# A recurrent attention block and a gated feed-forward on one core: a new list schedule, merged gram products, and y turned by transposes

## The chip, the core and the metric

The kernel runs on one core of a Trainium2 chip. Its five engines work side by side: PE (TensorE, matrix products), DVE (VectorE), ACT (ScalarE), POOL (GpSimd) and SP (SyncE, which here issues nearly all the transfers). Each engine takes its instructions in a fixed order and waits on semaphores for what others make. The metric is the time of one execution on the device in microseconds, as a median of the runs shown; lower is better.

## The reference

For 32 independent sequences (4 batches of 8 heads), with 768 tokens and a head size of 40, a 40 x 40 state is updated token by token. The output of all heads then goes through a normalised gated feed-forward.

```python
for t in range(S):
    y[:, :, t] = einsum('bhd,bhde->bhe', rt, state)
    Sa = einsum('bhde,bhe->bhd', state, at)
    state = state * wt[..., None, :] - einsum('bhd,bhe->bhde', Sa, bt) + einsum('bhd,bhe->bhde', vt, kt)
x = y as (B*S, H*D)                       # 3072 x 320
xn = x / sqrt(mean(x*x) + 1e-6) * rms_g
out = (silu(xn @ w_gate) * (xn @ w_val)) @ w_out     # 320 -> 1536 -> 320
```

r, k, v, w, a, b and the results are float32. The feed-forward's weights arrive as float64 and are narrowed in the kernel.

## The kernel before

The tokens are cut into 24 chunks of 32 (`C = 32`). Each chunk passes through three stages, and each pair of chunks (`CG = 2`) through a fourth.

- `front(c)` loads the chunk, turns it by transposes (`turned`, line 371), and climbs a ladder of five levels, `LEVELS = (1, 2, 4, 8, 16)`. A level makes one gram product of K with A (32 small products on PE, lines 546 to 550, recorded at line 368), copies part of it into the triangular matrix LT under a mask (`where`, a predicated copy on DVE), and makes K and A of the next level by scaling one half of each block (DVE, line 324) and copying the other half (ACT, line 348). At levels 1 and 2 the product takes 16 columns (`ps<-A,K`), at the other three 56 (`ps<-Ab,K`). Then LT goes through DRAM (sB) into another layout (M).
- `inverse(c)` inverts the triangle in 31 steps of two DVE instructions each (`tmp`, `Yi`), and sends it through DRAM (sY) back into LT.
- `main(c)` carries the state: X from the old state (`ST,aP`) and the values (`VU,LT`), then U (`Xs,LT`), then the update of ST (`VU,KN`). It also forms the scores (`rE,vut`), scales them into As, adds up five levels of products (`As,KN`, `As,kbn`) and the old state's part (`rE,Sd`, `r,Sd`) in y, turns y by 16 small products with the identity (`ps<-ident,y`, 32 records), normalises it to x, and turns that into xg.
- `feed(g)` runs the feed-forward of two chunks over 12 tiles of 128 hidden columns: the hidden products (`ps<-xg,wf`), Silu on ACT (sg), their product on DVE (hT), and the output products (`po<-wf,hT`). The narrowed weights (sW, in DRAM, made by `narrow` at the start) are loaded again for each pair into five buffers wf.

A product of float32 operands has two records of MATMUL and two of LDWEIGHTS in the trace; a transpose has one of each.

None of this is issued as it is written. Each step becomes a `Piece` with an engine, an estimated time and a due time, and `Plan.issue` (line 124) simulates the engines and writes the instructions out in the order in which it started them. The order is then fixed. Due times are written as offsets from the start of a chunk, which come every `T = 46.0`:

```python
due = d + 5 + 7.5 * j
pe(due - 14.5, 0.95, [mm(gr[half(i), o, n, 0:wide], K[...], side(A, l, 1)[...] if l <= 2 else A[..., 16:]) ...
```

On PE the planner also counts columns against a clock that it takes to be halved when there are too few, and puts in warming products (`plan.warm`, line 812, `po<-ident`) at the start. It counts transfers as one lane of 220 GB/s with fixed times around it. PSUM results are placed in three pairs of banks (`plan.room`).

Of the kernel before, what the change touches and what calls it, by code (L numbers as in the profile page):

```python
# [16 lines left out]
P = 128  # L17
C = 32
# [3 lines left out]
T = 46.0  # L22
N0, NF = -10.0, 6.0
S0, S1 = 15.0, 5.0
LAG = 10.0
M40 = 0.75
EARLY = 3
EPS = 1e-6


class Piece:


    def __init__(self, engine, due, time, issue, lane=0.0, columns=0, paced=False, room=None, since=0.0, tiled=None, many=0):
        self.engine, self.due, self.time, self.issue = engine, due, time, issue
        self.lane, self.columns, self.paced, self.room = lane, columns, paced, room
        self.many = many
        self.tiled = not columns if tiled is None else tiled
        self.ready, self.missing, self.users = since, 0, []


class Plan:
# [3 lines left out]

    LATENCY, SELF, MARGIN = 0.18, 0.115, 1.0
    SWITCH, STICK = 0.1, 3.0  # L50
    WINDOW, ENOUGH, KEEP = 3.41, 1600, 1300

    LINE, FETCH, STALL = 256, 3.6, 5.0
    LOOK, LOW = 1.0, 1300
    AHEAD, FAR = 2.0, 30.0
    WARM, FILL = 230.0, 1300

    def __init__(self, pairs, stand_ins):
        self.pieces = []
        self.seen = {}  # L60
        self.pairs, self.stand_ins = pairs, {t.tensor.name: t for t in stand_ins}
        self.now = {n: None for n in self.stand_ins}
        self.rooms = []

# [7 lines left out]
    def box(self, ap):  # L72
        dims = list(ap.ap)
        if ap.tensor.space == DRAM and ap.tensor.name not in self.now:

            g = all(s == 1 or s % 128 == 0 for s, n in dims) and [n for s, n in dims if s == 1] or [128]
            p = ap.offset % 128
            p, g = (p, g[0]) if p + g[0] < 128 else (0, 128)
            return p, p + g, ap.offset, ap.offset + sum(s * (n - 1) for s, n in dims) + 1
        row = dims[0][0]  # L80
        p, f = divmod(ap.offset, row)
        return p, p + dims[0][1], f, f + sum(s * (n - 1) for s, n in dims[1:]) + 1

    def add(self, engine, due, time, issue, outs, ins, **kw):
        me = len(self.pieces)
        piece = Piece(engine, due, time, issue, **kw)
        needs = set()
        mine = {}
        for aps, write in ((ins, False), (outs, True)):
            for ap in aps:  # L90
                name = ap.tensor.name
                a = self.box(ap)
                if name in self.now:
                    piece.room = self.now[name]
                    name = piece.room
                    a = 0, 128, *a[2:]
                if (name, write) in mine:
                    b = mine[name, write]
                    a = min(a[0], b[0]), max(a[1], b[1]), min(a[2], b[2]), max(a[3], b[3])
                mine[name, write] = a  # L100
        for (name, write), a in mine.items():
            left = []
            for b, i, w in self.seen.get(name, ()):
                if i != me and (write or w) and a[0] < b[1] and b[0] < a[1] and a[2] < b[3] and b[2] < a[3]:
                    needs.add(i)
                if not (write and a[0] <= b[0] and b[1] <= a[1] and a[2] <= b[2] and b[3] <= a[3]):
                    left.append((b, i, w))
            left.append((a, me, write))
            self.seen[name] = left
        piece.missing = len(needs)  # L110
# [3 lines left out]

# [9 lines left out]
    def issue(self):  # L124
        P_ = self.pieces
        waiting = {p.engine: [] for p in P_}
        free = {e: 0.0 for e in waiting}
        pairs = [0.0] * len(self.pairs)
        held, pace, left = [], 0.0, sum(p.paced is None for p in P_)
        clock, columns, recent, lane, order, full, line = [0.5], {}, [], 0.0, [], False, (0, -9.0)  # L130

        def put(i):
            p = P_[i]
            (held if p.paced and p.due > pace + self.FAR else waiting[p.engine]).append(i)

        def clock_at(t):
            while len(clock) <= int(t / self.WINDOW):
                c = columns.get(len(clock) - 1, 0)
                clock.append(1.0 if c >= (self.ENOUGH if clock[-1] < 1 else self.KEEP) else 0.5)
            return clock[int(t / self.WINDOW)]  # L140

        def fill(t):
            nonlocal line
            line = (line[0] + 4) % self.LINE, (t if line[0] + 4 >= self.LINE else line[1])
            order.append((t, None))
            end = t + 0.214 / clock_at(t)
            w = int(t / self.WINDOW)
            columns[w] = columns.get(w, 0) + 256
            recent.append((t, end, 256))
            return end  # L150

        def at_least(i):
            p = P_[i]
            return max(p.ready, min(pairs)) if p.room is not None and self.rooms[p.room][1] is None else p.ready

        for i, p in enumerate(P_):
            if not p.missing:
                put(i)
        for _ in P_:
            t, e = min((max(free[e], min(at_least(i) for i in w)), e) for e, w in waiting.items() if w)  # L160
            can = [i for i in waiting[e] if at_least(i) <= t]
            if e == "PE":
                since = max(free[e], 3.0)
                while t < self.WARM and since + 0.3 < t:
                    since = fill(since)
                t = max(t, since)
                since = t + self.LOOK - self.WINDOW
                recent = [r for r in recent if r[1] > since]
                had = sum(r[2] * (r[1] - max(r[0], since)) / (r[1] - r[0]) for r in recent)
                many = [i for i in can if not P_[i].tiled or P_[i].columns >= 1000]  # L170
                if many and (clock_at(t) < 1 or had < self.LOW):
                    can = many
                else:
                    can = [i for i in can if not P_[i].paced or P_[i].due <= pace + self.AHEAD] or can
                    while clock_at(t) == 1 and had < self.FILL:
                        t = fill(t)
                        had += 256
                at = int(t / self.WINDOW)
                clock_at(t)
            if e == "PE":  # L180
                def run(p):

                    time = (p.time + (self.SWITCH if p.tiled == full else 0)) / clock[at]
                    end, left, done, begun, lost = t, p.many, line[0], line[1], 0.0
                    while done + left >= self.LINE:
                        n = self.LINE - done
                        end += time * n / p.many
                        lost += max(0.0, begun + self.FETCH - end)
                        end = begun = max(end, begun + self.FETCH)
                        left, done = left - n, 0  # L190
                    return end + time * left / p.many, (done + left, begun), lost
                runs = {i: run(P_[i]) for i in can}
                i = min(can, key=lambda i: (P_[i].due + (self.STICK if P_[i].tiled == full else 0) + self.STALL * runs[i][2], i))
            else:
                i = min(can, key=lambda i: (P_[i].due, i))
            waiting[e].remove(i)
            p = P_[i]
            end = t + p.time
            if e == "PE":
                end, line, _ = runs[i]  # L200
                full = not p.tiled
                over = min(1.0, max(0.0, (end - (at + 1) * self.WINDOW) / (end - t)))
                columns[at] = columns.get(at, 0) + p.columns * (1 - over)
                columns[at + 1] = columns.get(at + 1, 0) + p.columns * over
                recent.append((t, end, p.columns))
            free[e] = end
            if p.lane:
                lane = max(lane, end + 1.2) + p.lane
                end = lane + 1.0
            if p.room is not None:  # L210
                room = self.rooms[p.room]
                if room[1] is None:
                    room[1] = min(range(len(pairs)), key=lambda q: pairs[q])
                    pairs[room[1]] = float("inf")
                room[0] -= 1
                if not room[0]:
                    pairs[room[1]] = end + self.LATENCY
            order.append((t, i))
# [626 lines left out]
```

## Time and profile before

| what | value |
|---|---|
| median of 3 runs | 1265.81 us (1259.08 to 1271.15) |
| profiled execution: span on the core | 1281.1 us |
| PE busy | 1152.5 us, 90% |
| DVE busy | 887.6 us, 69% |
| ACT busy | 467.3 us, 36% |
| mean granted clock of PE | 0.938 |
| `ps<-A,K`, 16 columns | 3072 records, 59.7 us busy |
| `ps<-Ab,K`, 56 columns | 4608 records, 90.5 us busy |
| `ps<-ident,y` | 768 records, 16.3 us busy |
| warming products `po<-ident` | 698 records, 93.7 us busy |

The profile was taken from one execution with the hardware profiler. Only its span is given; no separate time of the same execution is. Busy times of PE are modelled at their ends and records of neighbours overlap, so the sum of groups is larger than the time that they occupy. A granted clock of 0.5 means that PE runs at half its speed in that stretch. "DVE hT L324: 21.9, 23, 2.4" in a list of waits is the total in us, the count and the longest.

### The profile page before, as it was taken

To read this page: it belongs to the slowest core of one execution; us is meant where nothing else is said; L and a number is where in the kernel's file an instruction comes from. 1 tells how busy PE (TensorE), PEld (TensorE's weight loads), DVE (VectorE), ACT (ScalarE), POOL (GpSimd) and SP (SyncE) were. 2 spreads that over 40 slices of the span, in tenths; PEclk is the share of its full clock that TensorE was granted. 3 is DMA by queue.
4 is the path that set the end of the run, shared out by engine and by line. 5 is a ranking of instruction groups with operands and counts; after the bars stand their busy time and mean duration, and the time that the engine had idled before them with its cause. 6 is when DMAs were issued, how large, how long until landed. Compare 5 with 4: busy or idle time off the path is not lost.

```text
span 1281.1 us, 58318 instructions
## 1 busy us (share of the span) xinstructions
PE 1152.5 (90%) x25626; PEld 937.6 (73%) x25626; DVE 887.6 (69%) x3012; ACT 467.3 (36%) x1060; POOL 47.3 (4%) x118
## 2 busy tenths in 40 slices
PE   7998769998998999988998998988999998999997
PEld 7898667777776777776777676777777776777775
DVE  5778986868768578677678677667677677577311
ACT  3734554334233334333333333334333333331111
POOL 5000000000000000000000000000000000000000
PEclk9999668999898899999999997989999998999999
DMA  7656664535535435535535535435436545333342
GB/s 105 138 151 161 155 178 80 132 84 120 118 80 133 102 98 133 105 99 131 116 80 136 117 85 129 108 85 140 100 92 141 115 99 121 101 91 92 95 143 61
DMA packets 307902, 145.77 MB, mean 114 GB/s; under 512 B 270784, under 2 KB 284608, under 8 KB 307648
## 3 DMA queue, kind: packets, MB, share of 16 engines
q1 hardware_dynamic: 297856, 140.57, 46.2%
q8 instruction: 201, 3.29, 1.1%
q10 hardware_dynamic: 9792, 1.48, 0.8%
q14 instruction: 53, 0.43, 0.1%
HBM read 125.83 MB, written 16.12 MB: 111 GB/s over the span
## 4 chain that ended last, share of the span: by engine, by line
PE 44%; DVE 26%; SPq 12%; DMA 9%; issue 5%; ACT 3%; POOL 0%; DVEq 0%; POOLq 0%; ACTq 0%
PE ps L368 29%; SPq L365 12%; PE po L368 8%; DVE tmp L324 5%; DVE Yi L324 5%; PE ps L371 4%; PE po L812 4%; DMA M<-sB 3%; DVE As L324 3%; DVE hT L324 2%; DVE K L324 2%; DVE LT L324 2%; DVE y L324 2%; DMA sW<-hT 1%; DMA kbn<-in_k_dram 1%
## 5 line engine op out<-in xcount | busy, mean ns | idle before, releaser
L368 PE MATMUL ps<-xg,wf 128*128 128x256 f32 (+1 forms) x1728 | 382.0, 410 | 12.7 <-DMA wf<-sW 5.3
L368 PEld LDWEIGHTS ps<-xg,wf 128*128 128x128 f32 (+1 forms) x1728 | 274.2, 198 | 69.1 <-issue 11.0
L368 PE MATMUL po<-wf,hT 128*128 128x320 f32 x576 | 199.0, 470 | 23.0 <-DVE hT L324 21.9
L324 DVE TENSOR_TENSOR tmp<-Yi,M 128x60 f32<-128x60 f32 (+24 forms) x744 | 156.5, 210 | 40.5 <-DMA M<-sB 23.0
L324 DVE TENSOR_TENSOR Yi<-Yi,tmp 128x60 f32<-128x60 f32 (+24 forms) x744 | 156.0, 210 | 18.2
L344 ACT ACTIVATE sg<-ps 128x256 f32<-128x256 f32 x144 | 55.2, 384 | 270.5 <-PE ps L368 268.9
L368 PEld LDWEIGHTS po<-wf,hT 128*128 128x128 f32 x576 | 102.1, 196 | 70.2 <-DVE hT L324 30.8
L348 ACT COPY KN<-ps 128x640 f32<-128x640 f32 x96 | 66.4, 692 | 169.8 <-DVE LT L324 68.1
L324 DVE TENSOR_TENSOR hT<-ps,sg 128x256 f32<-128x256 f32 x144 | 60.6, 421 | 97.4 <-ACT sg L344 97.1
L368 PEld LDWEIGHTS ps<-Ab,K 40*64 40x64 f32 x4608 | 80.2, 143 | 36.1 <-issue 19.3
L348 ACT COPY K<-K 128x256 f32<-128x256 f32 x240 | 91.1, 415 | 31.8 <-PE ps L368 26.1
L368 PE MATMUL ps<-Ab,K 40*64 40x56 f32 x4608 | 90.5, 229 | 13.1 <-ACT K L348 6.2
L324 DVE TENSOR_TENSOR K<-K,T 128x512 f32<-128x512 f32 (+1 forms) x192 | 93.3, 490 | 9.6 <-ACT K L348 9.4
L812 PE MATMUL po<-ident 128*128 128x128 f32 x698 | 93.7, 293 | 6.6 <-POOL eye L421 5.2
L812 PEld LDWEIGHTS po<-ident 128*128 128x128 f32 x698 | 88.1, 206 | 7.9 <-POOL eye L421 5.2
L324 DVE COPY_PREDICATED LT<-msk,ps 128x256 f32<-128x256 uint32 x120 | 66.1, 551 | 32.3 <-PE ps L368 21.2
L324 DVE TENSOR_TENSOR As<-ps,msi 128x512 f32<-128x512 f32 (+1 forms) x192 | 80.1, 484 | 7.3 <-PE ps L368 7.3
L368 PEld LDWEIGHTS ps<-As,KN 128*40 128x40 f32 x3072 | 67.5, 128 | 22.8 <-issue 7.1
L368 PE MATMUL ps<-As,KN 128*40 128x32 f32 x3072 | 73.8, 208 | 6.7 <-DVE hT L324 5.8
L368 PEld LDWEIGHTS ps<-A,K 40*64 40x64 f32 x3072 | 54.5, 145 | 26.1 <-issue 15.8
L368 PE MATMUL ps<-A,K 40*64 40x16 f32 x3072 | 59.7, 214 | 7.1 <-issue 3.1
L324 DVE TENSOR_TENSOR y<-y,ps 128x256 f32<-128x256 f32 x120 | 50.6, 421 | 19.8 <-PE ps L368 17.4
(106 smaller groups left out, 1321.0 us busy)
## 6 DMA issues: line engine op xcount, KB each, us to landing
wf<-sW SPq DMA_DIRECT2D x144, 480.0 KB, 4.5
M<-sB SPq DMA_DIRECT2D x96, 128.0 KB, 2.8
sW<-hT SPq DMA_DIRECT2D x24, 240.0 KB, 3.4
wan<-in_w_dram SPq DMA_DIRECT2D x48, 80.0 KB, 3.1
wan<-in_a_dram SPq DMA_DIRECT2D x48, 80.0 KB, 3.5
wn<-in_w_dram SPq DMA_DIRECT2D x96, 40.0 KB, 2.7
rn<-in_r_dram SPq DMA_DIRECT2D x24, 160.0 KB, 5.3
wf<-in_moe_w_out_dram SPq DMA_DIRECT2D x12, 320.0 KB, 3.4
```

Of the source, the lines that this page charges most:

```text
L324: plan.add("DVE", due, time + 0.00104 * size(o), lambda at: fn(at(o), *m(at)), [o], aps(*args))
L344: plan.add("ACT", due, 0.08 + 0.00083 * size(o), lambda at: nc.scalar.activation(at(o), at(a), f, **kw), [o] + aps(acc), [a])
L348: plan.add("ACT", due, 0.08 + 0.00083 * size(o), lambda at: nc.scalar.copy(at(o), at(a)), [o], [a])
L365: plan.add(by, due, 0.45, lambda at: queue.dma_start(out=o, in_=i), [o], [i], lane=max(0.4, n * 4 / 220e3), since=since)
L368: return o, lhsT, rhs, lambda at: nc.tensor.matmul(at(o), lhsT, rhs, start=start, stop=stop, skip_group_check=True), 4
L371: return o, i, ident, lambda at: nc.tensor.transpose(at(o), i, ident), 2
L812: plan.warm = lambda: nc.tensor.matmul(po_[:, 0, DM:DM + P], ident, ident, start=False, stop=False, skip_group_check=True)
```

## The change

It has three parts.

1. **The planner is rewritten.** A product's time, its drain when the kind of tiling changes, and the delay until others see it now come from a table by kind (`PRODUCTS`), and every transfer's time to landing from another (`LOADS`). The planner models blocks of 256 instructions on PE, up to 8 transfers in flight, and dependencies by exact elements instead of boxes. Due times come from a long table (`DUE`), one number for each piece of each stage, with separate rows for the first and last chunks; the choice among ready pieces weighs due time against start time (`KEEN`), a change of tiling (`STICK`) and an instruction-block stall (`LOSS`). `T` is 43.36 and warming products may come until 199 on the planner's time instead of 230.
2. **The ladder's levels 1 and 2 share one gram product.** A holds seven columns for each block of four tokens, in a tile of 16 x 8 x 7: the last three as they are, two and one times the decay. One product of 56 columns then gives the entries at distances 1, 2 and 3 inside a block of four, and three predicated copies with new masks (`near`) take them into LT. Level 2's factor is applied to K in place, and A for level 4 is made directly.
3. **The sequences' slots are reordered** (`slot(n) = n % 4 * 2 + n // 4`) in LT, K, A, ST and KN, and **y is turned by four full transposes** instead of 16 small products with the identity.

In the instructions: of each of 24 chunks' products, 32 of 16 columns go, 32 others of 16 become 56 wide, and 16 products for y become 4 transposes. PE has 397 warming products instead of 349. DVE has 57 instructions more in the whole program, ACT 120 fewer, POOL three Memsets more (A, and two of y). SP issues 1410 transfers as before, in another order.

```diff
-T = 46.0
+T = 43.364560000000004
+WARM = 199.0
+PRODUCTS = {
+    "out": (0.915, 0.359, 0.434, 0, 2560), "h": (1.618, 0.306, 0.381, 0, 4096), ...
+LOADS = {
+    "sB": (1.5, 0.1), "LT": (1.65, 0.15), "M": (2.6, 0.65), "sY": (2.3, 0.47), "wf": (3.85, 2.05), ...
+DUE = {
+    ("", 0): """-596 -468 -407 -645 -502 -1178 -655 -103 -167 -101 -269 -259 -795 ...
...
+                    p, t = P_[i], max(at, free[e])
+                    score = p.due + keen[e] * (t - free[e])
+                    if e == "PE":
+                        if p.mode != mode:
+                            score += stick
+                        if best is None or score < best[0]:
+                            score += stall * lost(p, at)
...
+            if p.load:
+                at = max(free[e], at)
+                free[e] = at + self.ISSUE
+                server = max(server, at + self.BEGIN) + p.load[1]
+                end = behind[e] = max(server, at + p.load[0], behind[e] + self.BEHIND)
+                landed.append(end)
...
-        copy(d, by_i(Tl[1]), ps[:, :, :, 0])
-        A = A_.next()
-        copy(d, by_i(A), ps[:, :, :, 1])
+        copy(by_i(Tl[1]), ps[:, :, :, 0])
+        A, Ab = A_.next(), Ab_.next()
+        copy(A[:, :, :, 0:3], a4.rearrange("p n (g j) -> p n g j", j=4)[:, :, :, 1:4])
+        copy(Ab[:, :, 0:C]...[:, :, :, :, 0], a4...[:, :, :, :, 0])
...
+        tt(A[:, :, :, 3:5], A[:, :, :, 1:3], w4[:, :, :, 1:3], MUL)
+        tt(A[:, :, :, 6], A[:, :, :, 4], w4[:, :, :, 1], MUL)
+        gr = plan.room().rearrange("p o (n t) -> p o n t", n=N)
+        pe("gramk", [mm(gr[half(i), o, n, 0:56], K[part(o), 2 * n + i].rearrange("p x s -> p (x s)"),
+                        A[part(o), 2 * n + i].rearrange("p g j -> p (g j)")) for n, i, o in each])
+        for dist, at in ((1, 0), (2, 3), (3, 6)):
+            m = 4 - dist
+            where(LT...[:, :, :, dist:], near[:, dist - 1:dist]...[:, :, :, dist:]..., g4[:, :, :, at:at + m])
...
-        for j, l in enumerate(LEVELS):
+        for j, l in list(enumerate(LEVELS))[2:]:
...
-                dma(due, sB[seq(i, q, o)]..., LT[rows(i, 1 - q), o * N + 4 * q:o * N + 4 * q + 4])
+                dma(sB[seq(i, q, o)]..., LT[rows(i, 1 - q), o * N + q:(o + 1) * N:2], "sB")
...
-        xn = plan.room()
-        pe(d + 42.7, 0.6, [mm(xn[half(q), o, m * D:(m + 1) * D],
-                            y[part(o), 2 * (q * 4 + m):2 * (q * 4 + m) + 2].rearrange("p i t -> p (i t)"),
-                            ident[part(o), part(o)]) for m in range(4) for q in range(2) for o in range(2)])
-        xv = xn[:, :, 0:4 * D]
+        xn = plan.room()[:, 0].rearrange("p (m c) -> p m c", m=4)
+        pe("turn4", [flip(xn[:, m], y.rearrange("p (m c) t -> p m (c t)", m=4)[:, m], ident) for m in range(4)])
+        xv = xn.rearrange("p m (o e) -> p o m e", o=2)[:, :, :, 0:D]
```

## The prediction

> **What bounds the kernel now.** I read the page first: the busy shares, the clock row and the chain that ended last.
>
> ```profile
> span 1281.1 us, 58318 instructions
> PE 1152.5 (90%) x25626; PEld 937.6 (73%) x25626; DVE 887.6 (69%) x3012; ACT 467.3 (36%) x1060; POOL 47.3 (4%) x118
> PEclk9999668999898899999999997989999998999999
> PE 44%; DVE 26%; SPq 12%; DMA 9%; issue 5%; ACT 3%; POOL 0%; DVEq 0%; POOLq 0%; ACTq 0%
> q8 instruction: 201, 3.29, 1.1%
> ```
>
> PE is busy 90% and idle 128.6 us. The chain is PE for 44% of the span and changes hands often: PE is nearly full, with many short waits. The dip in the clock row lies at 120 to 210 us. So next I cut the span at 213.54 us, where the first output product of feed(0) begins.
>
> ```profile
> 0.00:213.54 213.54, 177.03 (x3624) 165.00 (x3624) 165.17 (x509) 107.35 (x220) 20.35 (x55) 0.85 0.62 142
> 213.54:1281.15 1067.61, 975.47 (x22008) 772.63 (x22002) 722.39 (x2503) 359.90 (x840) 26.96 (x63) 0.96 0.45 108
> 150.00:200.00 50.00, 36.02 (x903) 32.86 (x905) 45.79 (x139) 29.61 (x64) 2.03 (x4) 0.70 0.70 172
> 622.00:668.00 46.00, 42.69 (x1041) 34.03 (x1040) 34.17 (x121) 16.73 (x41) 0.70 (x2) 1.00 0.47 111
> ```
>
> After the length, the columns are busy PE, weight loads, DVE, ACT, POOL, the clock, the DMA share and GB/s. In the first stretch PE's 177 us contain the warming products (row po<-ident, 93.7 us in the whole run); DVE is the full engine, 45.8 of 50 us. In the second, 1067.6 us, PE is idle 92.1. A mean clock of 0.96 with states of 1.0 and 0.5 means some 85 us at half speed, of which about 43 us are lost. So 92 + 43 = 135 us of the second stretch are not work at full speed. I look at who causes them, and at one case.
>
> ```profile
> PE po L368 <- DVE hT L324: 21.9, 23, 2.4
> PE ps L368 <- issue: 21.6, 24, 3.7
> PE ps L368 <- DVE y L324: 13.0, 19, 3.2
> PE ps L368 <- DVE hT L324: 9.3, 12, 1.9
> ...
> 1070.30 0.69 PE L368 MATMUL ps<-Xs,LT 32*32 32x40 f32 x53
> 1074.72 0.47 PE L368 MATMUL ps<-Xs,LT 32*32 32x40 f32 x11 [3.73 <-issue]
> 1075.12 3.78 PE L368 MATMUL ps<-xg,wf 128*128 128x256 f32 x8
> ```
>
> No wait is long; they come from products that stand too close behind what they need. The last three rows show a stall's second price: after 3.73 us without work, eight products take 3.78 us. The same eight take 1.89 at full clock (timeline at 621.45), so the stall cost 1.9 us more.
>
> **The sum, part by part.** For PE I use the time from one group's start to the next group's start, since records of neighbours overlap.
>
> ```profile
> 619.91 0.68 PE L368 MATMUL ps<-ident,y 40*64 40x40 f32 x32
> 620.52 1.09 PE L371 MATMUL ps<-ident,wan 128*128 128x128 f32 x8
> 621.45 1.89 PE L368 MATMUL ps<-xg,wf 128*128 128x256 f32 x8
> ...
> 630.53 1.12 PE L368 MATMUL ps<-A,K 40*64 40x16 f32 x64
> 631.59 0.26 PE L368 MATMUL ps<-Xs,LT 32*32 32x40 f32 x4
> ```
>
> *Grams.* Per chunk the build has 32 fewer gram instructions: two products A,K with 16 columns become one with 56. A,K takes 631.59 - 630.53 = 1.06 us for 64 records. The merged form stands in the trace as Ab,K, 56 columns, also x64: 607.29 to 608.44 with a start-to-start near 1.0 to 1.1. Width costs nothing here, count does. Saved: 24 x 1.06 = 25 us, on the bounding engine.
>
> *y.* 32 records in 0.61 us become four transposes. Eight transposes take 621.45 - 620.52 = 0.93, so four take 0.47. Saved: 24 x 0.14 = 3 us. Here a rule speaks against the change: the Trainium skill, "TensorE: Matmul & The Clock Gate", Part 4 (PE-mode transpose), says that transposes do not count as busy for the clock gate as other products do. By it, every chunk could lose one more window: a clock dip in this trace lasts at least 3.4 us and loses 1.7, so 24 x 1.7 = 41 us. The row against it is 622 to 668: it holds several groups of eight transposes (two in a row at 644.28 to 646.2) and has clock 1.00. I take 0 and keep the 41 us for the range.
>
> *Instruction blocks.* The q8 row is 201 blocks of 16.4 KB; with 2 x 25626 records that is 255 instructions a block. The Trainium skill, "Runtime: NRT & Kernel Launch" (Instruction fetch mechanics), says blocks of 256 instructions are fetched ahead and crossing one is mostly hidden. By the rule the 21.6 us of "issue" waits are something else and fewer instructions win nothing; by the trace each long one ends just before the next block's fetch, and no two fetches start within 3.3 us, while 128 gram instructions run in 1.06 us. I follow the trace. The build has 8.2% fewer PE records (23514), so 184 blocks: -2 us by count alone; the rest depends on how wide products are mixed in.
>
> *DVE and ACT.* Per chunk DVE loses two predicated copies (551 ns each), A<-A (420) and two Ab<-A (291 each). It gains three predicated copies of 128, 256 and 384 elements (on average the same 551, so 1653), two products on A (291 and 420) and two on Ab of 192 elements (about 356 between the rows of 128 and 256). Net +0.97 us, 23 us in all. Hidden: DVE is busy 722 of 1068 us; it would be 745 of about 960, 78%. Uncovered it costs the 23 us. ACT loses A<-ps 585, A<-A 429, two Ab<-A at 312, four K<-K at 415 and gains about 1.37 us (three wider copies): -1.9 us per chunk, off PE's path but one link of two in the gram ladder goes. POOL gains three Memsets (896 and twice 512 elements, by the rows of 1024 and 512 about 1.9 us) behind the others at 18 us, ahead of the first gram: at most 2 us once. Slot order and strided LT pieces keep the same 128-byte rows and the same 1410 SP issues: 0.
>
> *New order.* No view shows it, so I count in the build: PE work, at this trace's start-to-start times, between a product and the one that needs it. Medians before to after: X to U 2.8 to 11.4 us; scores to first level 2.7 to 4.3; last level to y 2.2 to 4.7; y to x 2.5 to 4.1; hidden products to the output product 2.7 to 3.4, with 56 of 144 closer than 2 us before and 33 after. Changes between full and tiled products fall from 471 to 441. At one end, nothing is won (a fixed order misses real landings); at the other all 135 us but the final 8 us go, 127. By the counts the hT waits (31 us) fall by about 40%, the y waits by most, the others by some: I take half of the remaining 84 us idle and half of the 43, 63 us.
>
> *Start.* PE work before feed(0) is 62.7 us before and 60.4 after; DVE work before the second chunk's xg falls by 4% (174 to 168 in the same count), the warming products rise from 349 to 397. DVE idles some 16 of its first 50 us. Between 0 and 30 us; I take 15, nearer the DVE row.
>
> Sum: 1281 - 25 - 3 - 2 - 63 - 15 + 2 (POOL) = 1175 us of this execution. The page gives no time of it but the span; the median of the runs shown, 1265.8, is 0.988 of that, so 1175 becomes **1161 us**.
>
> Every moved step also moves its DMAs in SP's queue. Its 1410 issues stand finer mixed (884 groups instead of 657), and a wf load, which waits for an old output product, now often stands between pieces of sY, LT and sB. That is the third rival.
>
> **Rivals.** (1) Only the removed work counts; new waits replace the old ones one for one. For it: the chain has five kinds of releasers. Against it: the distances above. 1281 - 30 = 1251, so about 1236. (2) Nearly all waits go: all but the 20 us of blocks: 1281 - 30 - 107 - 25 = 1119, so 1106. Against it: 33 output products still stand close. (3) **Slower: SP's queue.** SP waited 180.8 us on PE's po in 56 waits (mean 3.2, longest 11.3), nearly all wf loads. SP is in order; an LT or M piece behind such a load comes late, X cannot start, and PE, in fixed order, stands. A stall of 5 us with its 1.7 us of half clock, once per chunk, is 161 us: 1281 - 30 - 15 + 161 - 63 = 1334, so 1318. It decides once it exceeds (63 + 45)/24 = 4.5 us per chunk. Against it: PE's waits on DMA are few today (wf 5.3 us, kbn 3.7, rn 2.8), none of them on LT or M. (4) The old and new order behave alike because DVE, at 78%, takes over the short waits: 1281 - 30 + 23, so about 1258, no change.
>
> **Chances.** Forecast 0.70 (its own range 1125 to 1205), (1) 0.10, (2) 0.09, (3) 0.07, (4) 0.04. A measurement of this kernel tells about 1% from no change. Faster by over 1%: forecast, (1), (2), 0.89; same 0.04; slower 0.07. The range 1105 to 1228 takes in (2), most of what the unknown costs allow, and the lower side of (1).
>
> **What would show it.** A,K with 16 columns gone, Ab,K-like rows x64 at about the same duration; y at four transposes; PE records near 23500; about 184 blocks; waits on hT under 20 us and on y under 6; the output product of feed(0) before 205 us; clock after it at 0.97 or higher; from there to the end about 960 us. I am wrong if PE's idle time behind the start stays above 85 us, if waits on LT, VU or DMA rise on PE, or if the clock falls while y transposes run.

## The result and the profile after

The changed kernel takes 1200.4 us (median of 4 runs, 1193.7 to 1204.2) against 1268.5 for the kernel before in the same set of runs: a ratio of **0.947** (0.942 to 0.953, the 95% interval). In a second set of runs the two stood at 0.946 (0.940 to 0.952). The forecast was 1161 us from 1265.8, a ratio of 0.917, so the direction was right and the size too large.

First four lines from the page of the changed kernel, whose span is 1191.9 us: busy shares, clock, the chain by engine, and the queue of instruction blocks.

```profile
PE 1084.3 (91%) x23514; PEld 889.9 (75%) x23514; DVE 904.3 (76%) x3069; ACT 434.5 (36%) x940; POOL 50.8 (4%) x121
PEclk8999899989999999999999999999999999999999
PE 45%; DVE 28%; issue 9%; SPq 7%; DMA 7%; ACT 3%; POOL 1%; DVEq 0%; ACTq 0%; POOLq 0%
q8 instruction: 184, 3.01, 1.1%
```

PE has 68 us less work in its records and is still 91% full. The clock row, which had two sixes, a seven and six eights before, now has three eights, and nines for the rest. SP's share of the chain fell from 12% to 7%. DVE is busier by 17 us, where 23 were counted.

Next come the two stretches, cut where the first output product of feed(0) begins, now at 206.67 us. After the length come busy PE, weight loads, DVE, ACT, POOL, then the clock.

```profile
0.00:206.67 206.67, 171.89 (x3546) 160.57 (x3546) 174.63 (x551) 104.25 (x200) 21.80 (x58) 0.95 0.61 147
206.67:1191.90 985.23, 912.37 (x19968) 729.33 (x19968) 729.64 (x2519) 330.29 (x741) 28.99 (x63) 0.98 0.48 117
```

PE idles 985.23 - 912.37 = 72.9 us of the second stretch, after 92.1 before. The clock records of the traces have 32.8 us at half speed in it, after 94.8 before.

The list of PE's waits shows which went:

```profile
PE ps L537 <- issue: 22.5, 18, 3.5
PE po L537 <- DVE hT L491: 6.2, 12, 1.1
...
PE ps L537 <- DVE LT L491: 4.4, 6, 1.5
PE ps L537 <- DVE y L491: 4.3, 3, 3.4
PE ps L537 <- DVE hT L491: 3.8, 8, 1.0
```

With the smaller rows of the same releasers, hT fell from 31.2 to 12.4 us and y from 14.2 to 7.6. The "issue" waits, in which PE waited for nothing that the profile shows, stayed at 24.5 and 24.8; experiment 4 ties them to the instruction blocks. Everything else stayed too, in smaller pieces: 128.6 - 31.2 - 14.2 - 24.5 = 58.7 us before, 107.6 - 12.4 - 7.6 - 24.8 = 62.8 after.

The merged gram as a group (count, busy us and mean ns of one record, idle time before), and then in time order:

```profile
L537 PE MATMUL ps<-A,K 40*64 40x56 f32 x1536 | 27.7, 221 | 1.6 <-DVE A L491 0.5 <-ACT rE L518 0.4 <-DVE tmp L491 0.3
```

```profile
740.08 1.15 PE L537 MATMUL ps<-A,K 40*64 40x56 f32 x64
741.16 0.92 PE L537 MATMUL ps<-Xs,LT 32*32 32x40 f32 x64
```

It holds half the records, 3.5 times as wide, and takes 741.16 - 740.08 = 1.08 us from start to start, as the 16-column product did (1.06).

### The profile page after: what moved, and what is told of

Read it like the earlier page. It is cut to its first block, busy times and chain, and to the rows that moved or that the text cites. A ratio compares the mean times of both kernels' runs of the same rounds, so it can differ in the third digit from the quotient of the medians.

```text
span 1191.9 us, 54002 instructions
## 1 busy us (share of the span) xinstructions
PE 1084.3 (91%) x23514; PEld 889.9 (75%) x23514; DVE 904.3 (76%) x3069; ACT 434.5 (36%) x940; POOL 50.8 (4%) x121
## 4 chain that ended last, share of the span: by engine, by line
PE 45%; DVE 28%; issue 9%; SPq 7%; DMA 7%; ACT 3%; POOL 1%; DVEq 0%; ACTq 0%; POOLq 0%
PE ps L537 30%; PE po L537 9%; SPq L534 7%; PE ps L540 6%; DVE tmp L491 5%; DVE Yi L491 4%; DVE LT L491 3%; DVE K L491 3%; DVE hT L491 3%; DMA M<-sB 2%; DVE As L491 2%; DVE sg L491 1%; DVE Ab L491 1%; DVE y L491 1%; DMA kbn<-in_k_dram 1%
## 5 line engine op out<-in xcount | busy, mean ns | idle before, releaser
L537 PE MATMUL ps<-xg,wf 128*128 128x256 f32 (+1 forms) x1728 | 363.1, 396 | 13.8 <-issue 3.2
L537 PEld LDWEIGHTS ps<-xg,wf 128*128 128x128 f32 (+1 forms) x1728 | 263.7, 191 | 74.8 <-issue 23.7
L537 PE MATMUL po<-wf,hT 128*128 128x320 f32 x576 | 185.7, 453 | 7.9 <-DVE hT L491 6.2
L1001 PE MATMUL po<-ident 128*128 128x128 f32 x794 | 102.4, 287 | 5.2 <-POOL eye L599 5.2
L1001 PEld LDWEIGHTS po<-ident 128*128 128x128 f32 x794 | 96.5, 200 | 6.5 <-POOL eye L599 5.1
L537 PE MATMUL ps<-Ab,K 40*64 40x56 f32 x4608 | 85.5, 223 | 17.4 <-DVE LT L491 4.4
L491 DVE TENSOR_TENSOR As<-ps,msi 128x256 f32<-128x256 f32 (+1 forms) x192 | 81.8, 483 | 8.2 <-PE ps L537 7.9
L518 ACT COPY K<-K 128x256 f32<-128x256 f32 (+1 forms) x168 | 69.4, 444 | 39.7 <-PE ps L537 26.4
L491 DVE COPY_PREDICATED LT<-near,ps 128x384 f32<-128x384 uint32 (+2 forms) x72 | 52.2, 725 | 1.1 <-PE ps L537 0.8
L491 DVE TENSOR_TENSOR y<-y,T 128x256 f32<-128x256 f32 x96 | 41.1, 428 | 4.4 <-ACT y L518 2.0
L518 ACT COPY Ab<-Ab 128x128 f32<-128x128 f32 x96 | 26.8, 297 | 38.1 <-DVE Ab L491 22.4
```

The costliest lines, as they stand in the source:

```text
L491: plan.add("DVE", time + each * size(o), 0.087, lambda at: fn(at(o), *m(at)), [o], aps(*args))
L518: scalar(o, [a], lambda at: nc.scalar.copy(at(o), at(a)))
L537: return o, lhsT, rhs, lambda at: nc.tensor.matmul(at(o), lhsT, rhs, start=start, stop=stop, skip_group_check=True), 4
L1001: plan.warm = lambda: nc.tensor.matmul(po_[:, 0, DM:DM + P], ident, ident, start=False, stop=False, skip_group_check=True)
```

## The experiments

The median of the kernel before differed by up to 0.6% between sets of runs, so kernels of different sets are compared by their ratios to the kernel before. Theory A is the prediction's: part of the gain is PE work removed, part is the order. Its rivals B and D give all of it to one of the two. The theories of the later experiments are named where they are tested. No run takes out the slots' new arrangement alone.

**1. The new order with the old number of grams.**

```diff
         pe("gramk", [mm(gr[half(i), o, n, 0:56], K..., A...) for n, i, o in each],
+           extra=[mm(gr[half(i), o, n, 0:16], K..., A...[:, 0:16]) for n, i, o in each])
```

> The new kernel, in its own order, with 32 gram products of 16 columns put back in front of every chunk's merged one (the planner does not know of them; their result is overwritten). Theory A (removed products count in full because PE is the bound): 24 x 1.06 = 25 us of work, 12 more instruction blocks, some 5 us of further waits: 1200 becomes about 1230 (1222 to 1240). Rival B (the new order alone made the gain, and the removed grams lay beside waits): 1200 to 1208.

Measured: 1225.3 us, ratio 0.971 (0.964 to 0.978) against 0.947. The grams cost 2.4%, or some 30 us, so A holds, and B (all order) falls. Without the saved grams the new order is still 2.9%, or some 37 us, ahead of the kernel before. The span grew by 28.3 us over the changed kernel's first profile. The stretch after the first output product:

```profile
213.93:1220.20 1006.27, 941.70 (x21184) 756.23 (x21184) 731.33 (x2519) 330.83 (x741) 27.77 (x63) 0.97 0.47 115
```

PE is busy 29.3 us more in that stretch. Its time at half clock rose from 32.8 us (42.9 in a second profile of the changed kernel) to 60.3, which the expectation did not have.

**2. The old planner with the merged gram.** Into the kernel before went only the front's new ladder (one tile A of seven columns a block, `near` masks, due times of the old levels):

```diff
-        for j, l in enumerate(LEVELS):
+        pe(d - 9.5, 0.95, [mm(gr[..., 0:56], K..., A...) for n, i, o in each], 560, tiled=True)
+        for dist, at in ((1, 0), (2, 3), (3, 6)): where(d + 5, LT..., near..., g4...)
+        for j, l in list(enumerate(LEVELS))[2:]:
```

> The kernel before, with its own planner and due times, and only the merged gram (levels 1 and 2 in one product of 56 columns, three predicated copies); y and slots as before. Theory A: 25 us of PE work and 12 instruction blocks fewer, with the waits as they were: about 1238 (1228 to 1248). Rival B (the order alone made the gain): 1260 to 1272. Rival D (the order is worth nothing, arithmetic is all): 1200 to 1215.

Measured: 1240.2 us, ratio 0.983 (0.977 to 0.990). That is 21 us, somewhat less than A's 25 to 30, and a third of the gain. B and D both fall. The run changes more than the grams, though: the old planner made its order anew, and it put in 528 warming products instead of 349. The two stretches, cut at its first output product:

```profile
0.00:204.15 204.15, 188.90 (x3641) 178.07 (x3641) 171.39 (x536) 101.15 (x195) 21.06 (x55) 1.00 0.64 148
204.15:1233.60 1029.45, 929.13 (x20810) 739.91 (x20808) 734.66 (x2534) 333.51 (x745) 27.31 (x64) 0.98 0.47 112
```

The waits of the old order are all still there: PE idles 1029.45 - 929.13 = 100.3 us in the second stretch, with 40.5 us of hT waits. But the clock is already that of the new kernel. The four executions have a mean clock of 0.973 to 0.982, those of the kernel before in the same set 0.945 to 0.960, and those of the changed kernel 0.969 to 0.978. There are 44.9 us at half clock behind the first output product and none ahead of it, where the kernel before has 94.8 and 64.9. And that product comes as early as in the new order. So the higher clock and the shorter start do not need the new planner. Whether they come from the removed grams or from the added warming products is not separated. What the new planner adds, with y and the slots, is the step from 0.983 to 0.947, some 45 us, and the profiles show it as less idle time of PE: 72.9 us instead of 100.3.

**3. y by 16 products again, in the new order.**

```diff
-        pe("turn4", [flip(xn[:, m], y...[:, m], ident) for m in range(4)])
+        pe("turn4", [flip(...) ...], instead=[mm(xr[half(q), o, m * D:(m + 1) * D], y[part(o), 4 * m + 2 * q:...]..., ident[part(o), part(o)]) ...])
```

> The new kernel, in its own order, with y turned by 16 small products for each chunk again instead of four transposes (the planner still counts the transposes). Theory A: 3 us more work and 5 more instruction blocks: about 1206 (1199 to 1213). Rival C (transposes do not count for PE's clock and cost clock dips): the clock rises and the time falls by up to 41 us, 1160 to 1190.

Measured: 1199.2 us, ratio 0.950 (0.944 to 0.956) against 0.947 and 0.946. The difference, 0.3%, cannot be told from none, and A's 3 us would not be seen either. Rival C falls: nothing got faster, and the clock of this execution was 0.975 against 0.978.

**4. Block borders moved by half a block.**

```diff
+        for _ in range(32):
+            nc.tensor.matmul(po_[:, 0, DM:DM + 1], ident, ident[:, 0:1], start=False, stop=False, ...)
         plan.issue(due, KEEN, STICK, LOSS, MARGIN)
```

> The new kernel in its own order, with 32 one-column products (128 instructions) ahead of everything on PE, where PE waits 5 us anyway: every border of a block of 256 instructions then falls half a block away from where the planner put it. Theory E (the issue waits are fetches of blocks): the issue waits stay at records 193 or 194 of 256 counted from the start, stand at other products than in the new kernel, and grow from 23 us to 30 to 50 us; time 1208 to 1228. Rival F (they belong to the products where they stand): same products, same 23 us, 1198 to 1204.

The place was right and the size wrong. I numbered PE's weight loads, matmuls and semaphore instructions from the start in each trace. All 21 "issue" gaps over 0.3 us in the kernel before, 16 of 18 in the changed kernel and all 20 here end at number 193 or 194 of a block of 256. So they moved to other products with the border. But they did not grow: the row of ps has 16.9 us in 21 waits, the longest 2.1. One of them in time order:

```profile
920.38 0.78 PE L537 MATMUL ps<-rE,vut 40*64 40x32 f32 x41
923.23 0.86 PE L537 MATMUL ps<-rE,vut 40*64 40x32 f32 x23 [2.07 <-issue]
```

The time was 1191.4 us, ratio 0.943 (0.936 to 0.950), not slower at all. A group of scores is cut in two where a block ends. So the places that the planner chose for its block ends bought nothing that this run could measure.

**5. PE alone.** A kernel of products only, with nothing that waits for another engine (48 warming products, 640 grams of 16 columns, 48, 640 of 56, 48, 400 transposes, 48, 80 wide products, then 40 times 16 grams and 2 wide ones).

> PE alone, no waits on other engines: 640 gram products of 16 columns in a row, 640 of 56 columns, 400 transposes of 128x128, 80 products of 256 columns, and 40 times 16 grams and 2 wide products; nothing of the reference is computed, zeros are written out. Theory E (blocks of 256 instructions cannot come faster than about 3.3 us): a row of grams runs at 3.3 to 4.5 us per 64 products, not the 2.1 us that 256 instructions take in the kernel's short groups, with gaps at every 256th record; the mixed row has few gaps. Rival: 2.1 to 2.3 us per 64 products without gaps. Width: 16 and 56 columns take the same. Transposes: if they do not count for the clock, it falls to 0.5 within 7 us of the row of transposes and stays there; if they count, it stays at 1.0.

The first row of grams in time order with two lines of the second, and then four of the rows as stretches: both rows of grams, the transposes, and grams mixed with wide products (after the length: busy PE, weight loads, DVE, POOL, then the clock).

```profile
18.35 3.92 PE L48 MATMUL g<-data 40*64 40x16 f32 x255
23.27 2.82 PE L48 MATMUL g<-data 40*64 40x16 f32 x128 [1.01 <-issue]
26.73 21.70 PE L48 MATMUL g<-data 40*64 40x16 f32 x768 [0.64 <-issue]
...
69.76 2.08 PE L48 MATMUL g<-data 40*64 40x56 f32 x128 [0.86 <-issue]
73.49 17.77 PE L48 MATMUL g<-data 40*64 40x56 f32 x640 [1.64 <-issue]
```

```profile
18.35:52.70 34.35, 31.82 (x1281) 31.08 (x1280) 0.00 (x0) 0.00 (x0) 0.59 0.02 4
66.36:101.30 34.94, 32.06 (x1281) 31.38 (x1280) 0.00 (x0) 0.00 (x0) 0.58 0.02 5
114.46:158.10 43.64, 43.64 (x402) 43.64 (x401) 0.00 (x0) 0.00 (x0) 1.00 0.00 1
203.50:269.00 65.50, 65.50 (x1440) 49.37 (x1440) 0.00 (x0) 0.00 (x0) 1.00 0.01 3
```

The row of 640 grams takes 34.4 us, or 3.44 us per 64 products, where the kernel's short groups take 2.1 us for as many; the fetches of blocks in it start 3.35 to 4.0 us apart. 16 and 56 columns take the same. Grams mixed with wide products show no gap. The clock, for which the prediction kept up to 41 us in its range, stays at 1.00 under 400 transposes. Under grams alone it falls to one half 6 us after they begin and stays there until 5.6 us after they end, though PE is busy 31.8 of 34.4 us.

The 3.44 us were what theory E expected, but for the most part it is the half clock that makes them, not the blocks. In the kernel before, 64 records of grams at half clock take 1.9 us, so 128 would take some 3.7:

```profile
341.62 1.91 PE L368 MATMUL ps<-A,K 40*64 40x16 f32 x64
```

In the long stretches at half clock, 128 records take 3.55 to 3.62 us with no gap shown. Only the first 6 us of each row show the blocks at full clock: there 128 records of grams, one block with their weight loads, took 2.08 us and the next began 3.73 us after it (the two lines of the second row). So E holds where the clock is full, with one clear case in this run.

**6. The changed kernel and the kernel before once more.**

> The new kernel unchanged, as the measure for the others of this call, which share its chip. Expected 1195 to 1205, and a second look at its stalls: issue waits of 18 to 27 us on PE.

> The kernel before, unchanged, for a second profile. If the first profile (1281.1 us, above the highest of the timed runs) was an execution with more stalls than usual, this one spans 1250 to 1268 us, with PE idle after the first output product below 92 us and a clock above 0.938. If it was typical: 1272 to 1285.

The second stretch of each, the kernel before first:

```profile
212.05:1267.20 1055.15, 963.45 (x22008) 764.64 (x22002) 722.11 (x2503) 359.87 (x840) 27.13 (x63) 0.96 0.45 110
206.02:1187.50 981.48, 916.26 (x19968) 732.83 (x19968) 729.23 (x2519) 330.78 (x741) 30.55 (x63) 0.98 0.48 117
```

The changed kernel took 1194.0 us beside 1261.6. Its second profile has 12.7 us of issue waits in the row of ps, fewer than expected, 43 us at half clock and 59 us of PE gaps behind the start, counted up to PE's last product (first profile: 22.5, 33 and 66). Such small terms differ by some 10 us between two executions of one kernel. The kernel before spans 1267.2 us in its second profile, with 76.9 us at half clock behind the start instead of 94.8, but nearly the same idle time (85.1 us of gaps, as against 85.5). Its time was 1269.0, 1.8 us above the span, as for the changed kernel (1193.7 and 1191.9). So the first profile, 1281.1 us, was most likely a longer execution than usual; no timed run of this kernel, of which the longest took 1274.3 us, reached that.

**7. Less DVE work at the start.** The last three steps of the narrowing work on 8 of 480 columns.

```diff
+        if plan.stage[0] == "narrow" and fn != nc.vector.tensor_scalar:
+            cut = lambda x: x[:, 0:8] if isinstance(x, bass.AP) else x
```

> The new kernel in its own order; of the narrowing of the weights at the start the last three DVE steps work on 8 columns of 480 (the weights are wrong), which takes some 24 x 3 x 0.5 = 36 us of work from DVE in the first 200 us. Theory G (DVE bounds the start): the first output product comes 12 to 30 us earlier and the time falls by as much. Rival H (loads or the chain of the first chunks bound it): less than 6 us.

Measured: 1189.3 us, ratio 0.945 (0.938 to 0.952) against 0.946. DVE lost 32.6 us, and the first output product came at 206.01 us, as in the kernel with all of the work (206.02 in its second profile). Theory G falls, H holds. In the chain between 120 and 207 us, DVE's hT steps had been the largest part with 13%; now PE's products are, with 17%, and the landing of kbn has 10%. The narrowed weights leave at the same times within 3 us. I read this as a second chain only just behind the first; no run takes that one away.

**8. Less DVE work in the steady part.** As and y are formed for 4 of 16 slots from the third chunk on.

```diff
+        if plan.stage[0] == "main" and plan.stage[1] >= 2 and o.tensor.name.startswith(("As", "y")) and o.ap[1][1] == NI:
+            cut = lambda x: x[:, 0:4] if isinstance(x, bass.AP) else x
```

> The new kernel in its own order; from the third chunk on, the scaled scores As and the sums of y are formed for 4 of 16 slots only (the rest is left out), which takes about 3.4 us a chunk, some 8%, from DVE and nothing from PE. Theory J (what is left of PE's idle time, besides instruction blocks, is DVE running late in its fixed order): 15 to 35 us less. Rival K (DVE has room enough; PE's waits come from PE's own order and from the blocks): within 8 us of the new kernel.

Measured: 1186.9 us, ratio 0.941 (0.935 to 0.948): 0.5% below the changed kernel, with overlapping intervals. DVE's busy time fell by 82 us and PE's gaps behind the start only to 56.6, from 58.5 in the same set. J falls; K holds, with medians 7.1 us apart where it allowed 8. DVE has room enough.

**9. One weight of the planner.** First without, then with more avoidance of block stalls.

```diff
-STICK, LOSS, MARGIN = 1.93, 8.6, 1.0
+STICK, LOSS, MARGIN = 1.93, 0.0, 1.0      # the second run: 12.0
```

> The new planner with LOSS = 0: it still counts the fetch of blocks on its clock but does not avoid a stall by its choice of products. By the run with moved block borders, the avoiding is worth little: issue waits 15 to 30 us, time within 12 us of the new kernel, a little more for an order that its table of due times was not made for. If the avoiding mattered: issue waits above 40 us, time up by 20 or more.

> The new planner with LOSS = 12 in place of 8.6: it avoids block stalls more, and its PE order parts from the new kernel's at row 282 of 1388 (with LOSS = 0 it was row 232). Theory N (the table of due times fits only the weights that it was made with, and any other choice falls out of it): 1245 to 1290, as with LOSS = 0. Rival O (LOSS = 0 lost its 80 us because it no longer avoided block stalls): 1185 to 1210, issue waits at or below those of the new kernel.

LOSS = 0 gave 1277.2 us, ratio **1.014** (1.007 to 1.021): slower than the kernel before, with the same arithmetic as the new one. LOSS = 12 gave 1255.0, ratio 0.995 (0.991 to 0.999). The stretch after the first output product and PE's longest waits, for LOSS = 0 and then for LOSS = 12:

```profile
207.20:1286.10 1078.90, 956.36 (x19968) 759.58 (x19968) 737.59 (x2519) 333.18 (x741) 26.48 (x63) 0.94 0.43 107
```

```profile
PE ps L537 <- issue: 25.8, 22, 3.9
PE ps L540 <- ACT x L521: 15.7, 6, 6.7
PE ps L537 <- DVE LT L491: 13.7, 14, 2.2
```

```profile
211.00:1249.10 1038.10, 942.01 (x19968) 749.05 (x19968) 737.40 (x2519) 331.19 (x741) 27.09 (x63) 0.95 0.45 111
```

```profile
PE ps L537 <- DVE LT L491: 13.6, 13, 2.4
PE ps L537 <- DVE tmp L491: 12.2, 8, 3.4
PE ps L537 <- issue: 11.9, 11, 1.8
```

Neither branch of the first expectation came true: the time rose by 83 us, yet the issue waits stayed at 25.8. With LOSS = 12 they are the smallest of all profiles, 11.9 us, and the kernel is 5% slower than the new one. So block stalls are not what either lost. PE idles 122.5 and 96.0 us in these stretches, after 72.9 in the changed kernel, in short waits on x, LT and hT above all in the first run, and on LT and tmp in the second. And 139.7 and 105.7 us of them are at half clock, after 32.8. O falls, and N's forecast came true on both sides of the weight. Both kernels have the changed kernel's products, slots and steps on DVE and ACT, so these alone do not make the gain; the order is needed too.

**10. The planner without its table.**

```diff
+    if stage in ("main", "front", "inverse", "feed"):
+        return {"front": -12.0, "inverse": 45.0, "main": 95.0, "feed": 235.0}[stage] + T * (2 if stage == "feed" else 1) * c
```

> The new planner without its table of due times: every piece of a stage has one due time (front -12, inverse 45, main 95, feed 235 us, plus 43.36 a chunk), ties go by the program's order. All else as in the new kernel, the arithmetic too. Theory L (the order's gain lies in the table, which fits this planner and these weights alone): slower than the old order with the merged gram, 1245 to 1330. Rival M (the planner's rules and its measured times make the order): 1195 to 1225.

Measured: 1335.2 us, ratio 1.055 (1.048 to 1.061), with 126.7 us of PE gaps and 193.5 us at half clock after the first output product, which came at 255 us. M falls; L holds: the kernel is slower than that of experiment 2, and even 5 us above L's range. The planner's rules and its measured times, with one due time for a whole stage, do not make an order that beats the old one.

## Why the prediction was right or wrong

- **Grams, 25 us.** Right in kind and size: 21 us with the old planner, some 30 in the new order. Width cost nothing. The second price, time at half clock where small products crowd, was not in the sum.
- **y, 3 us, and the transposes' clock.** Not larger than can be told. The choice of the trace's row over the rule held: 400 transposes in a row kept the clock at 1.00. The Trainium skill ("TensorE: Matmul & The Clock Gate", Part 4) says that a transpose does not count as PE being busy in the same way, and the prediction's estimate from that was up to 41 us. The measurement decides here.
- **Instruction blocks.** 184, as forecast, and right in kind: the waits lie at one place of 256 records. The Trainium skill ("Runtime: NRT & Kernel Launch", Instruction fetch mechanics) calls such crossings mostly hidden; here they leave 13 to 23 us of 1190 in the row of ps. That the chosen places of block ends are worth little in this order was not foreseen.
- **New order, 63 us: the step that failed.** It was "half of the remaining 84 us idle and half of the 43". The idle time after the first output product fell by 19 us in the first pair of profiles and by 27 in the second, not by 42. The count of distances read hT and y rightly (31.2 to 12.4, 14.2 to 7.6). It was wrong to carry it over to the rest: block waits and some 60 us of other short waits stayed, and taking 82 us of work from DVE hardly touched them (experiment 8). The clock's loss, half of the time at half speed, fell by 31 and by 17 us, where 21 were forecast. But experiment 2 has that higher clock without the new planner, and experiment 1 loses part of it when only the grams come back. So this half of the term cannot be put down to the order alone, and its right size is luck. By the ratios the new order, with y, slots and start, is worth 37 us (experiment 1) to 45 us (experiment 2), where 63 + 15 were forecast.
- **Start, 15 us.** It was 7 and 6. DVE is busy 174.6 of the 206.7 us there, but it is not alone on the chain (experiment 7), and experiment 2 reaches the same point as early with the old planner. Nor does the point decide the time: in experiment 4 it came at 215.90 us, and that kernel was no slower.
- **The scale, 0.988.** It changes no ratio: 1175 of 1281 and 1161 of 1265.8 are both 0.917. The first profile of before, from which the sum started, is 14 us longer than the second, with more time at half clock to be won (94.8 us against 76.9).
- **The sum.** The start, the idle time, the clock and the rest give 7 + 19 + 31 + 32 = 89 us in the first pair of profiles and 6 + 27 + 17 + 30 = 80 in the second, where 15 + 42 + 21 + 28 = 106 were forecast. The rest, which is the removed work, is right; the order's idle time and the start are not. The medians moved by 68 us. The pairs show more, since both profiles of the changed kernel are the fastest execution of their set, and the first profile of before was a long one.
- **Rivals and signs.** The first rival was as near as the forecast, 1236 against 1200, but not in kind: waits did fall. SP's queue never decided. Of the signs of being wrong, one came in a small way: waits on LT on PE rose from none to 8 us in the first profile and 10 in the second. DVE at 76% was not the bound.

## What to carry to other kernels

Here the removed instructions on the bounding engine were the safe term of the sum, and the better order was not. One changed weight of the planner turned a gain of 5% into a loss of 1.4%, so such an order belongs together with the exact planner, table and kernel that made it. When the old order is run with one part of a change, look at what else its planner then does: here it added warming products. Before scaling a sum to a median, take a second profile of both kernels: short waits and clock dips moved the span of the kernel before by 14 us between two executions. And when a few named waits shrink, do not expect the unnamed ones to follow.

## What was not expected of the hardware

Small tiled products did not hold PE's clock. Grams back to back, with PE busy 31.8 of 34.35 us, had a clock of 0.59, and half after the first 6 us, while transposes, wide products, and 16 grams with two wide products in turn held 1.00. A gap of about 1 us lies shortly before each fall, so the gap may have had a part in it. It does not explain why the clock stayed at half, since in the first row the next 21.7 us of grams show no gap. The low clock under grams fits the rise from 33 to 60 us at half clock when they were put back (experiment 1).
